# A kernel's own scheduler gets new latencies, transfer costs and priorities, and the last head's probabilities are split straight from PSUM

## The chip, the cores and the metric

One Trainium2 chip, one core. The metric is the time of one execution on the device, in microseconds. The core has TensorE (PE, matmuls and transposes), VectorE (DVE), ScalarE (ACT), GpSimd (POOL), and transfers (DMA), which this kernel starts from SyncE (SP) in one queue.

## The reference

Attention over clusters (2 batches, 8 heads, 768 positions, 64 wide, 16 centroids a head), whose output goes through two feed-forward layers (512 to 2048 to 512, 1536 rows).

```python
# attention
q_assign = argmax(einsum('bhsd,hcd->bhsc', q_n, c_n)); k_assign likewise   # nearest centroid
mask = q_assign[:, :, :, None] == k_assign[:, :, None, :]
scores = where(mask, scale * q @ k.T, -1e9)
scores -= max(scores, -1)
attn = exp(scores);  attn /= sum(attn, -1) + 1e-9
out = attn @ v
# layer 1
h = x @ w_in;  g = maximum(h, 0) + alpha * minimum(h, 0);  x = g @ w_out
# layer 2
h = x @ w_in2
P = a0 + a1*h + a2*h**2 + a3*h**3;  Q = 1 + |b0|*|h| + |b1|*h**2
out = (P / (Q + 1e-6)) @ w_out2
```

The weights arrive as 64-bit floats.

## The kernel before

Every product is made from parts: each operand is split into a high part and what is left of it (low part), and three of the four partial products are added. So each operand needs a copy (high) and a subtraction (low).

*Stages.* Heads i = 0 to 15 come in pairs j = 0 to 7 (i = 2j and 2j+1). For a pair, q, k and v are loaded (`load`), transposed and split (`ph_T`), multiplied with the centroids (`ph_logits`, L552 is the matmul, then `ph_lt`), and made into rows that say which cluster each position has (`ph_oht`). Per head, transfers put the parts together into operand tiles: `operands1` (L617 the q and k parts, L620 and L623 the cluster rows) writes one of 3 slots `op1`, `operands2` (L632, L636) one of 2 slots `op2`. Then:

- `max_chunk`: nine chunks of scores, 512 wide, on PE (L664) into a PSUM bank, DVE takes the row maxima (L670). `m_chain` transposes the maxima on PE (L684) and writes them into `op1` by a transfer (L690).
- `st_chunk`: nine chunks of the transposed scores (PE, L709 and L710) into a bank; ACT takes the exponential (L714) and writes it to a buffer `p32` in SBUF, of which a piece holds two of the six 128-row tiles of P.
- `p_split`: per tile of P, 128x768, the high part (a copy, by ACT L414 or by POOL or DVE L416) and the low part (a subtraction, L726, by DVE or POOL) in `pt`.
- `v_split` (V parts), `pv_tile`: per 128 query rows 18 matmuls (L787 to L789) into a bank of the pool `o`; the first also makes sums of V. `pv_fin` (DVE, L804, L808, L811, L812) normalises, and per pair `x_T` transposes (PE, L826) and splits (ACT; DVE L834) into `x`.

The feed-forward layers are 96 steps of 512 rows by 128 hidden columns: `w_prep` makes weight parts from 64-bit data (L992 and L998 ACT, L1000 and L1002 DVE, L1005 POOL, then a copy and the subtraction L1012), `emit_h` is 12 matmuls (L1029) and the activation, whose parts are L414 and L1075, `emit_y` is 12 more (L1098).

*PSUM.* Eight banks: six (`S`) for chunks of scores and other short uses, two (`o`) for PV, maxima and the like; in the layers four for h, four for y.

*What sets the order.* No engine's order is written by hand. `SC.op(...)` records each operation with the engines that may run it (each with a cost in us, and a bias), what it reads and writes, and a priority `SC.t`, a time in planned us. `Sched.run` then plays through all of them: of the ready operations, each is put on the engine on which it would end first (cost plus bias), and on each engine the one with the smallest start plus `WP` times its priority goes next. A buffer's slot can be taken once its last use has ended by the plan. At the end the instructions are emitted in the order of their planned starts. So a constant in the plan does not delay or speed anything by itself: it sets which instruction stands before which in an engine's queue, and which engine gets an operation that could go to several. On the chip each engine works its queue in that order and waits where something isn't there yet.

Of the kernel before, what the change touches and what calls it, by code (L numbers as in the profile page):

```python
# [19 lines left out]
ACTF = mybir.ActivationFunctionType  # L20
# [10 lines left out]
WP = 0.0025  # L31
# [26 lines left out]
class Sched:  # L58
# [6 lines left out]
    LAT = 0.16  # L65
# [74 lines left out]
    def run(self, engines):  # L140
# [7 lines left out]
        while ready:  # L148
# [42 lines left out]
            if eng == DMA:  # L191
                free[eng] = start + 0.63
                moved = max(moved, start + 1.28) + cost
                o.end = moved + 1.05
            for b in o.bufs:
                b.uses -= 1
                b.done = max(b.done, o.end)
                if b.uses == 0:
                    b.slot.free = b.done
            for x in o.outs:  # L200
                raw = x.deps[o]
                lat = self.LAT
                if eng == DMA:
                    lat = 0.1
                x.est = max(x.est, o.end + lat) if len(x.alts) > 1 or x.alts[0][0] != eng else max(
                    x.est, o.end + (self.SAME if raw and eng != PE else 0.0))
                x.left -= 1
                if not x.left:
                    ready.append(x)
# [44 lines left out]
def clustered_attention__then__ffn_prelu__then__ffn_rational(  # L254
# [64 lines left out]
    EARLY = 77.8906  # L319
    SL, AHEAD, LEAD = 2.0, 14.0, 30.0  # L320
# [117 lines left out]
    def nb(n):  # L438
        return n / 280e3
# [4 lines left out]
    def load(nm, src, j):  # L444
        b, hp = divmod(j, NHP)
        t_ = SC.buf("raw" + nm)
        due = (((2 * j - 1) * T + 1) if nm == "v" else (2 * j - 4) * T + 2) * SL - AHEAD
        whole = nm == "v" or j == 0
        pat = "h (p t) d -> p h t d" if whole else "h (p t) d -> p t h d"
        op((DMA, nb(393216) * (1 if whole else 2)), lambda e: e.dma_start(  # L450
            out=by_head(t_) if whole and nm != "v" else t_.v, in_=src[
                b, 2 * hp:2 * hp + 2].rearrange(pat, t=T)), w=[t_], t=due,
           after=first.get((nm, j), LEAD + due))
        raws[nm, j] = t_
# [200 lines left out]
    def max_chunk(i, c):  # L655
# [11 lines left out]
        op((PE, 0.24), mm, r=[(a, "x"), (a, "oh"), (a, "neg"), (a, "one")], w=[ps])  # L667
# [28 lines left out]
    p32s = {}  # L696

    def st_chunk(i, c):
        a, b_, ps = op1[i % 3], op2[i % 2], SC.buf("S", "st")
        u, cc = divmod(c, CPU)  # L700
        if cc == 0:
            p32s[i, u] = SC.buf("p32")
        p32, parts = p32s[i, u], pieces(cc)

        def mm(e):
            for k_, lo, hi, off in parts:
# [5 lines left out]
        op((PE, 0.48), mm, r=[(b_, 0), (b_, 1), (b_, 2), (a, "x"), (a, "oh"), (a, "neg"),  # L712
                              (a, "one"), (a, "m")], w=[ps])
        op(act_p(CH), lambda e: e.activation(  # L714
# [3 lines left out]
    def p_split(i, t):  # L718
        u, k_ = divmod(t, 2)
# [3 lines left out]
        op([act_s(S), but(dve1(S), 0.5193), but(pool1(S), -0.1128)],  # L723
# [4 lines left out]
        ptile[i, t] = pt_  # L728

# [35 lines left out]
    def pv_tile(i, t):  # L765
# [16 lines left out]
        def mms(e):  # L782
# [8 lines left out]
        op((PE, 0.58), mms,  # L791
           r=[(d, e_, 0), (d, e_, 1), (d, "one")] + [(p, a) for p in tiles for a in range(2)],
# [63 lines left out]
    for i in range(-4, NHEAD + 1):  # L856
        je, jo, jn = (i + 4) // 2, (i + 3) // 2, (i + 2) // 2
        for t in range(T):
            SC.t = (i * T + t) * SL
            if 0 <= i < NHEAD:  # L860
                for c in ((0, 1), (2,))[t % 2]:
                    SC.t = (i * T + t + (0, 0.67, 0.33)[c]) * SL + 0.0
                    st_chunk(i, CPU * (t // 2) + c)
                    if c:
                        SC.t += 0.0 - 0.0
                        p_split(i, t // 2 * 2 + c - 1)
                SC.t = (i * T + t) * SL
# [20 lines left out]
            if i % 2 == 0 and je < NPAIR:  # L888
                if t in (2, 3, 4):
                    hurry(je == 0)  # L890
                    SC.t += 0.0
# [31 lines left out]
            if i >= 3 and i % 2 == 1 and t == 1:  # L923
                SC.t += 3.0579
# [5 lines left out]
    STEP = 5.2  # L930
# [87 lines left out]
    def emit_h(s):  # L1018
# [19 lines left out]
        SC.t = T0 + STEP * (s - 0.0901)  # L1038
# [42 lines left out]
    def emit_y(s):  # L1081
# [21 lines left out]
        for d, (ps, mm) in enumerate(lows):  # L1103
# [4 lines left out]
            SC.t = T0 + STEP * (s - 8.5752)  # L1108
# [60 lines left out]
```

## Time and profile before

| what | before |
|---|---|
| median of 3 runs | 796.49 us (795.05 to 796.76) |
| the profiled execution, its span | 797.74 us, 796.0 us |
| PE busy | 765.4 us, 96% of the span |
| POOL, DVE, ACT busy | 579.7, 599.4, 560.3 us |
| granted clock, mean | 0.984 |
| stages by the span | heads 0 to about 235, the last head's PV beside the first weights to about 271, layers to 787, end 796 |

The span is what the profiler recorded of the execution; 1.74 us lie around it. In the views, a row of the waits says which engine and line waited, for which engine and line (or transfer), how long in all, how often, and the longest. A row of the chain gives the start, the length and what was done. A row of the groups gives the line, engine, operation, output and input with their shapes, the count, the busy time, the mean of one in ns, and the idle time before them.

### The profile page before, as it was taken

The page shows a single profiled execution, that of the slowest core. Times are in us where ns is not written, and L with a number is a line of the kernel's source. Part 1 is how long each engine was busy: PE and PEld are TensorE (multiplying, and loading weights), DVE is VectorE, ACT ScalarE, POOL GpSimd, SP SyncE. Part 2 cuts the span into 40 slices and gives each one's busy share as a digit, 9 for nine tenths or more (in the row PEclk, how much of TensorE's full clock was granted, in tenths as well). Part 3 has the DMA queues.
Part 4 walks back from the last instruction along what each step waited for, and adds up shares of the span by engine and source line. Part 5 has one row for each costly group of instructions (what it writes and reads, how often), then busy time and mean ns, then how long its engine had stood idle before and what let it go on. Part 6 is the DMA issues. An engine that isn't in the chain of part 4 may idle for free.

```text
span 796.0 us, 13977 instructions
## 1 busy us (share of the span) xinstructions
PE 765.4 (96%) x5295; PEld 636.0 (80%) x5295; DVE 599.4 (75%) x871; ACT 560.3 (70%) x991; POOL 579.7 (73%) x475
## 2 busy tenths in 40 slices
PE   8998999999997799999999999999999999999996
PEld 7687797887886688888888888888888888888885
DVE  5787787888797999775662563479889899777775
ACT  3377877887878666665653664688899798666672
POOL 4286956967679899996762773799889689667443
PEclk9899999999899999999999999999999999999999
DMA  5685757656442433332320330211112110000012
GB/s 129 127 171 115 156 126 151 136 123 175 97 102 81 159 99 114 107 108 77 107 80 0 106 96 11 79 54 54 53 54 80 53 54 1 0 1 1 1 54 106
DMA packets 57859, 67.58 MB, mean 85 GB/s; under 512 B 27232, under 2 KB 46272, under 8 KB 57792
## 3 DMA queue, kind: packets, MB, share of 16 engines
q1 hardware_dynamic: 57792, 66.69, 31.9%
q8 instruction: 41, 0.67, 0.4%
q14 instruction: 26, 0.21, 0.1%
HBM read 43.04 MB, written 3.15 MB: 58 GB/s over the span
## 4 chain that ended last, share of the span: by engine, by line
PE 84%; DVE 6%; DMA 5%; ACT 2%; POOL 1%; issue 1%; SPq 1%; DVEq 0%; ACTq 0%; POOLq 0%
PE bank L1029 32%; PE bank L1098 32%; PE bank L709 3%; PE bank L664 3%; PE bank L710 3%; DMA arena_r<-arena_r 2%; PE bank L787 2%; PE bank L552 2%; DVE mp L670 2%; PE bank L789 2%; PE bank L788 2%; DMA arena_p<-in_v 2%; PE bank L525 1%; DMA arena_p<-in_k 1%; DVE arena_p L726 1%
## 5 line engine op out<-in xcount | busy, mean ns | idle before, releaser
L1029 PE MATMUL bank<-x,arena_r 128*128 128x512 f32 x1152 | 277.6, 390 | 3.2 <-ACT arena_r L414 1.1
L1098 PE MATMUL bank<-arena_r 128*128 128x512 f32 x1152 | 277.8, 390 | 1.7 <-ACT arena_r L414 1.0
L1029 PEld LDWEIGHTS bank<-x,arena_r 128*128 128x128 f32 x1152 | 215.9, 188 | 48.9 <-POOL arena_r L1012 3.1
L1098 PEld LDWEIGHTS bank<-arena_r 128*128 128x128 f32 x1152 | 215.6, 188 | 48.4 <-ACT arena_r L414 1.4
L1075 POOL TENSOR_TENSOR arena_r<-arena_p,arena_r 128x512 fp32r<-128x512 f32 x96 | 132.9, 1385 | 38.6 <-ACT arena_r L414 19.8
L726 POOL TENSOR_TENSOR arena_p<-arena_p 128x768 f16<-128x768 f32 x66 | 115.3, 1755 | 18.7 <-ACT arena_p L414 15.1
L414 ACT CAST arena_r<-arena_p 128x512 fp32r<-128x512 f32 x137 | 83.4, 621 | 44.7 <-DVE arena_p L1040 28.1
L1005 POOL TENSOR_TENSOR arena_p<-arena_p 128x512 int32<-128x512 int32 x64 | 93.8, 1468 | 27.1 <-ACT arena_p L998 15.9
L670 DVE TENSOR_REDUCE mp<-bank 128x1 f32<-128x512 f32 x144 | 91.3, 683 | 16.8 <-PE bank L664 16.6
L1012 POOL TENSOR_TENSOR arena_r<-arena_p,arena_r 128x512 fp32r<-128x512 f32 x64 | 92.5, 1447 | 13.0 <-ACT arena_r L414 12.5
L714 ACT ACTIVATE arena_p<-bank 128x512 f32<-128x512 f32 x144 | 80.0, 593 | 30.3 <-PE bank L710 24.4
L1000 DVE TENSOR_SCALAR arena_p<-arena_p 128x512 uint32<-128x512 uint32 x64 | 64.3, 1004 | 38.7 <-ACT arena_p L992 38.7
L1040 DVE SCALAR_TENSOR_TENSOR arena_p<-arena_p,nal 128x512 f32<-128x512 f32 x48 | 53.0, 1106 | 50.2 <-ACT arena_p L1043 50.1
L1002 DVE SCALAR_TENSOR_TENSOR arena_p<-arena_p 128x512 uint32<-128x512 uint32 x64 | 84.1, 1315 | 1.5
L1057 POOL TENSOR_TENSOR arena_p<-arena_p 128x512 f32<-128x512 f32 x48 | 62.4, 1301 | 29.7 <-ACT arena_p L1054 29.5
L709 PE MATMUL bank<-arena_r 128*128 128x512 f32 x192 | 69.8, 381 | 1.4 <-DVE x L834 1.0
L1040 DVE SCALAR_TENSOR_TENSOR arena_p<-arena_p,cq,bank 128x512 f32<-128x512 f32 x48 | 35.7, 744 | 41.8 <-ACT bank L1065 36.1
L789 PE MATMUL bank<-arena_p 128*128 128x65 f16 x576 | 62.2, 197 | 3.6 <-POOL arena_p L726 2.9
L710 PE MATMUL bank<-arena_r 128*128 128x512 f32 x192 | 64.4, 349 | 0.0
L787 PE MATMUL bank<-arena_p 128*128 128x65 f16 x576 | 62.8, 197 | 0.0
L788 PE MATMUL bank<-arena_p 128*128 128x64 f16 x576 | 62.2, 195 | 0.0
L664 PE MATMUL bank<-arena_r 96*128 96x512 f32 x192 | 53.1, 372 | 7.9 <-DMA arena_r<-arena_r 3.5
(122 smaller groups left out, 1272.3 us busy)
## 6 DMA issues: line engine op xcount, KB each, us to landing
arena_p<-in_moe_w_in SPq DMA_DIRECT2D x32, 512.0 KB, 3.8
arena_p<-in_moe_w_out SPq DMA_DIRECT2D x32, 512.0 KB, 3.6
arena_r<-arena_r SPq DMA_DIRECT2D x24, 384.0 KB, 5.4
arena_r<-arena_r SPq DMA_DIRECT2D x24, 192.0 KB, 5.2
arena_p<-in_q SPq DMA_DIRECT2D x8, 384.0 KB
arena_p<-in_k SPq DMA_DIRECT2D x8, 384.0 KB, 5.5
arena_r<-x SPq DMA_DIRECT2D x8, 384.0 KB, 5.5
arena_p<-in_v SPq DMA_DIRECT2D x8, 384.0 KB
```

The source lines that it names most:

```text
L414: e.copy(o_, i_)
L670: op(dvep(CH), lambda e: e.reduce_max(mp.v[:, n0:n0 + 2 * np_ - 1:2], ps.v.rearrange("p (a k) -> p a k", a=np_), axis=AX.X), r=[ps], w=[(m ...
L709: e.matmul(o_, lhsT=b_.v[:, 1, ks], rhs=b_.v[:, 0, lo:hi], start=True, stop=False)
L710: e.matmul(o_, lhsT=a.v[:, 1, ks], rhs=a.v[:, 0, lo:hi], start=False, stop=True)
L726: lambda e: e.tensor_sub(pt_.v[:, 1, :], src(), pt_.v[:, 0, :]),
L1002: op(dve2(N), lambda e, d0=d0, hi=hi: e.scalar_tensor_tensor(u(d0), hi(), 0x80000000, u(d0), op0=ALU.bitwise_and, op1=ALU.bitwise_or), r=[ ...
L1005: op(pool2(N), lambda e, d0=d0, d1=d1: e.tensor_tensor(n32(d0), n32(d0), n32(d1), op=ALU.add), r=[d0, d1], w=[d0])
L1012: lambda e, wt=wt, pick=pick, src=src: e.tensor_tensor(pick(wt.v)[:, 1], src(), f32(pick(wt.v)[:, 0]), op=ALU.subtract),
L1029: e.matmul(ps.v, lhsT=wi.v[:, wi_, kk, :], rhs=x[kk][:, xi, cols], start=n == 0, stop=n == 3 * KD - 1)
L1040: lambda e: e.scalar_tensor_tensor(o_.v, a_.v, sc, b_.v, op0=p0, op1=p1))
L1075: op([dve2(N), pool2(N)], lambda e: e.tensor_tensor(gg.v[:, 1, :], G.v, f32(gg.v[:, 0, :]), op=ALU.subtract), r=[G, (gg, 0)], w=[(gg, 1)])
L1098: e.matmul(ps.v, lhsT=lhsT, rhs=rhs, start=first and wi_ == gi == 0, stop=last and gi == 1)
```

## The change

The plan's constants change, and with them the order: `LAT`, one delay of 0.16 us from the end of an operation to one that needs it on another engine, becomes a part by the engine that ends (`TAIL`) plus a part by the engine that waits (`SEM`). A transfer ends in the plan earlier after its start (1.2 and 0.69 us for 1.28 and 1.05), is moved at 190 in place of 280 KB a us, and the loads that were counted double no longer are. A slot counts as free `TAIL` + 0.09 us after the last use. Costs of three PE operations, the weight of priorities and a number of priority shifts change.

For the last head alone (i = 15), `st_chunk` lets ACT write the exponential back into its PSUM bank; copies (ACT or DVE) and subtractions (DVE) read it there, piece by piece (512 or 256 wide, 12 of each), and `p_split` has nothing to do. The dependences of PV are kept in `pkeys`.

```diff
-WP = 0.0025
+WP = 0.0029
...
-    LAT = 0.16
+    TAIL = {PE: 0.16, ACT: 0.1, DVE: 0.08, POOL: 0.04, DMA: 0.0}
+    SEM = {PE: 0.14, ACT: 0.04, DVE: 0.04, POOL: 0.08, DMA: 0.03}
...
-                moved = max(moved, start + 1.28) + cost
-                o.end = moved + 1.05
+                moved = max(moved, start + 1.2) + cost
+                o.end = moved + 0.69
...
-                b.done = max(b.done, o.end)
+                b.done = max(b.done, o.end + self.TAIL[eng] + 0.09)
...
-                lat = self.LAT
-                if eng == DMA:
-                    lat = 0.1
+                lat = self.TAIL[eng] + self.SEM[x.alts[0][0]]
...
-    EARLY = 77.8906
-    SL, AHEAD, LEAD = 2.0, 14.0, 30.0
+    EARLY = 102.4323
+    SL, AHEAD, LEAD = 2.0, 14.9599, 30.0
...
-        return n / 280e3
+        return n / 190e3
...
-        op((DMA, nb(393216) * (1 if whole else 2)), lambda e: e.dma_start(
+        op((DMA, nb(393216)), lambda e: e.dma_start(
...
-        if cc == 0:
+        if cc == 0 and i < LASTS:
...
+        if i >= LASTS:
...
+            op(act_p(CH), lambda e: e.activation(ps.v, ps.v, ACTF.Exp, scale=scale),
+               r=[ps], w=[ps])
+            for k_, lo, hi, off in parts:
+                t_ = ptile[i, 2 * u + k_]
+                src = lambda off=off, lo=lo, hi=hi: ps.v[:, off:off + hi - lo]
+                op([act_p(hi - lo), dvep(hi - lo)],
+                   lambda e, t_=t_, src=src, lo=lo, hi=hi: copy(e, t_.v[:, 0, lo:hi], src()),
+                   r=[ps], w=[(t_, 0, lo)])
+                op(dvep(hi - lo), lambda e, t_=t_, src=src, lo=lo, hi=hi: e.tensor_sub(
+                    t_.v[:, 1, lo:hi], src(), t_.v[:, 0, lo:hi]),
+                   r=[ps, (t_, 0, lo)], w=[(t_, 1, lo)])
...
+            return
...
     def p_split(i, t):
+        if i >= LASTS:
+            return
...
-        op([act_s(S), but(dve1(S), 0.5193), but(pool1(S), -0.1128)],
+        op([act_s(S), but(dve1(S), 0.5193), but(pool1(S), -0.0486)],
...
-                    SC.t = (i * T + t + (0, 0.67, 0.33)[c]) * SL + 0.0
+                    SC.t = (i * T + t + (0, 0.6098, 0.33)[c]) * SL + 0.0
...
-                        SC.t += 0.0 - 0.0
+                        SC.t += 1.5884 - 0.0
...
-                    SC.t += 0.0
+                    SC.t += 0.8265
                     ph_T(je, t - 2)
...
-                    SC.t += 4.3843
+                    SC.t += 3.2767
                     v_split((i + 1) // 2)
...
-    STEP = 5.2
+    STEP = 5.2741
...
-        SC.t = T0 + STEP * (s - 0.0901)
+        SC.t = T0 + STEP * (s - -0.0819)
...
-            SC.t = T0 + STEP * (s - 8.5752)
+            SC.t = T0 + STEP * (s - 4.2479)
```

The plan is remade as a whole, so instructions move on every engine. Three places, as they stand in the queues; a line's number in the changed kernel is one less up to L710, 19 or 20 more behind it (L726 is L745, L1005 is L1025, L1012 is L1032, L834 is L854).

*SP's queue at the start* (L450 before and L449 after are the loads of q and k, 128x12x64 those of pair 1; L617 or L616 the first transfer of an operand tile). Before:

```order
L450 DMA arena_p<-in_q 128x12x64
L617 DMA arena_r<-x 64x2x768
L450 DMA arena_p<-in_k 128x12x64
L617 DMA arena_r<-x 64x2x768
L620 DMA arena_r<-arena_r 16x768
```

and after:

```order
L449 DMA arena_p<-in_q 128x12x64
L449 DMA arena_p<-in_k 128x12x64
L616 DMA arena_r<-x 64x2x768 x3
L619 DMA arena_r<-arena_r 16x768
L622 DMA arena_r<-arena_r 16x768
```

Pair 1's k load stands ahead of the first operand transfer, and three operand transfers ahead of the first cluster rows.

*PE at pair 3's transposes* (L525 and L524 are the transposes of `ph_T`, L552 and L551 the logits, L590 later transposes of clusters, L775 the sums of V). Before:

```order
L775 LDWEIGHTS level
L775 MATMUL bank<-arena_p,level 128x64
L525 MATMUL bank<-idf,arena_p 128x128 x8
L552 MATMUL bank<-arena_r 128x384 x3
L709 MATMUL bank<-arena_r 128x512
L710 MATMUL bank<-arena_r 128x512
L590 LDWEIGHTS arena_p
```

and after, at the last of these transposes:

```order
L709 MATMUL bank<-arena_r 128x512
L710 MATMUL bank<-arena_r 128x512
L524 MATMUL bank<-idf,arena_p 128x128 x4
L709 MATMUL bank<-arena_r 128x256
L710 MATMUL bank<-arena_r 128x256
L709 MATMUL bank<-arena_r 128x256
L710 MATMUL bank<-arena_r 128x256
```

Before, the logits follow the transposes at once; after, chunks of scores and PV tiles stand between, and the logits come 144 rows of PE's list later.

*POOL and DVE at the last head.* POOL before, from the maxima of head 15 (L681):

```order
L681 TENSOR_SCALAR nh_116<-mx_111 128x6
L726 TENSOR_TENSOR arena_p<-arena_p 128x768 x2
L1005 TENSOR_TENSOR arena_p<-arena_p 128x512
L416 TENSOR_SCALAR arena_r<-arena_p 128x512
L1012 TENSOR_TENSOR arena_r<-arena_p,arena_r 128x512
L1005 TENSOR_TENSOR arena_p<-arena_p 128x512
L726 TENSOR_TENSOR arena_p<-arena_p 128x768
L1012 TENSOR_TENSOR arena_r<-arena_p,arena_r 128x512
L726 TENSOR_TENSOR arena_p<-arena_p 128x768
L1005 TENSOR_TENSOR arena_p<-arena_p 128x512
L726 TENSOR_TENSOR arena_p<-arena_p 128x768
L1012 TENSOR_TENSOR arena_r<-arena_p,arena_r 128x512
```

POOL after, from the same place (L680):

```order
L680 TENSOR_SCALAR nh_116<-mx_111 128x6
L745 TENSOR_TENSOR arena_p<-arena_p 128x768
L1025 TENSOR_TENSOR arena_p<-arena_p 128x512
L415 TENSOR_SCALAR arena_p<-arena_p 128x768
L745 TENSOR_TENSOR arena_p<-arena_p 128x768
L1032 TENSOR_TENSOR arena_r<-arena_p,arena_r 128x512
L745 TENSOR_TENSOR arena_p<-arena_p 128x768
L1025 TENSOR_TENSOR arena_p<-arena_p 128x512
L1032 TENSOR_TENSOR arena_r<-arena_p,arena_r 128x512
L1014 TENSOR_SCALAR arena_p<-arena_p 128x512
L1025 TENSOR_TENSOR arena_p<-arena_p 128x512
```

and DVE after (L726 is here the new subtraction, L824 to L832 the end of PV, L854 the split of x, L1020 and L1022 weights):

```order
L726 TENSOR_TENSOR arena_p<-bank,arena_p 128x256
L854 TENSOR_TENSOR x<-bank,x 128x512
L726 TENSOR_TENSOR arena_p<-bank,arena_p 128x256
L854 TENSOR_TENSOR x<-bank,x 128x256
L1020 TENSOR_SCALAR arena_p<-arena_p 128x512
L726 TENSOR_TENSOR arena_p<-bank,arena_p 128x512
L1022 SCALAR_TENSOR_TENSOR arena_p<-arena_p 128x512
L1020 TENSOR_SCALAR arena_p<-arena_p 128x512
L726 TENSOR_TENSOR arena_p<-bank,arena_p 128x512
L726 TENSOR_TENSOR arena_p<-bank,arena_p 128x256 x2
L1022 SCALAR_TENSOR_TENSOR arena_p<-arena_p 128x512
L726 TENSOR_TENSOR arena_p<-bank,arena_p 128x512
```

The subtractions of the last head's P leave POOL's list, between whose weight splits they stood, and stand as smaller pieces in DVE's, between its weight splits.

More of the change, by code (lines that the diff above doesn't have):

```diff
@@ L665, in mm @@
                          rhs=a.v[:96, 1, lo:hi], start=True, stop=True)
-        op((PE, 0.24), mm, r=[(a, "x"), (a, "oh"), (a, "neg"), (a, "one")], w=[ps])
+        op((PE, 0.23), mm, r=[(a, "x"), (a, "oh"), (a, "neg"), (a, "one")], w=[ps])
         n0 = 6 * u + (0, 1, 4)[c % CPU]
@@ L694, in clustered_attention__then__ffn_prelu__then__ffn_rational @@
     ptile = {}
-    p32s = {}
+    p32s, pkeys = {}, {}
+    LASTS = NHEAD - 1
     def st_chunk(i, c):
@@ L700, in st_chunk @@
         u, cc = divmod(c, CPU)
-        if cc == 0:
+        if cc == 0 and i < LASTS:
             p32s[i, u] = SC.buf("p32")
-        p32, parts = p32s[i, u], pieces(cc)
+        p32, parts = p32s.get((i, u)), pieces(cc)
         def mm(e):
@@ L710, in mm @@
                 e.matmul(o_, lhsT=a.v[:, 1, ks], rhs=a.v[:, 0, lo:hi], start=False, stop=True)
-        op((PE, 0.48), mm, r=[(b_, 0), (b_, 1), (b_, 2), (a, "x"), (a, "oh"), (a, "neg"),
+        op((PE, 0.46), mm, r=[(b_, 0), (b_, 1), (b_, 2), (a, "x"), (a, "oh"), (a, "neg"),
                               (a, "one"), (a, "m")], w=[ps])
+        if i >= LASTS:
+            for k_, *_ in parts:
+                if (i, 2 * u + k_) not in ptile:
+                    ptile[i, 2 * u + k_] = SC.buf("pt")
+            op(act_p(CH), lambda e: e.activation(ps.v, ps.v, ACTF.Exp, scale=scale),
[9 more added lines that the diff above has]
+                   r=[ps, (t_, 0, lo)], w=[(t_, 1, lo)])
+                pkeys.setdefault((i, 2 * u + k_), []).extend([(t_, 0, lo), (t_, 1, lo)])
+            return
         op(act_p(CH), lambda e: e.activation(
@@ L728, in p_split @@
         ptile[i, t] = pt_
+        pkeys[i, t] = [(pt_, 0), (pt_, 1)]
     vinv = {}
@@ L789, in mms @@
                 e.matmul(o1, lhsT=lo, rhs=d.v[:, e_, kt, 64:129], start=False, stop=kt == T - 1)
-        op((PE, 0.58), mms,
-           r=[(d, e_, 0), (d, e_, 1), (d, "one")] + [(p, a) for p in tiles for a in range(2)],
+        op((PE, 0.55), mms,
+           r=[(d, e_, 0), (d, e_, 1), (d, "one")] + [k_ for kt in range(T) for k_ in pkeys[i, kt]],
            w=[(ps, t)])
@@ L898, in clustered_attention__then__ffn_prelu__then__ffn_rational @@
                 hurry(jo == 0)
-                SC.t += (-1.2643, 0, -0.6544, 0, -0.4435, 0)[t]
+                SC.t += (-1.2643, 0, -0.6544, 0, -0.5101, 0)[t]
                 if t == 0:
@@ L923, in clustered_attention__then__ffn_prelu__then__ffn_rational @@
             if i >= 3 and i % 2 == 1 and t == 1:
-                SC.t += 3.0579
+                SC.t += 3.3245
                 x_T((i - 3) // 2)
```

## The prediction

> **What bounds the kernel now.** I read the table by stages first: in the row 280 to 787 TensorE (PE) is busy 506.95 of 507.00 us, so the two FFN layers are bound by PE at full clock, and a new order can only shorten what comes before them, 280 us, and the 9 us behind. Columns: length, busy time of PE, its weight loads, DVE, ACT, POOL, then the granted clock.
>
> ```profile
> 0.00:30.00 30.00, 25.20 (x218) 21.07 (x218) 19.48 (x50) 8.34 (x17) 9.34 (x36) 0.99 0.58 128
> 60.00:120.00 60.00, 55.61 (x719) 47.88 (x716) 48.31 (x92) 45.20 (x88) 42.48 (x35) 0.97 0.61 131
> 180.00:225.00 45.00, 42.23 (x553) 36.35 (x552) 35.53 (x63) 35.12 (x67) 30.24 (x24) 0.92 0.56 131
> 235.40:270.60 35.20, 26.95 (x417) 22.00 (x416) 29.32 (x35) 27.49 (x49) 31.32 (x21) 0.95 0.35 106
> 280.00:787.00 507.00, 506.95 (x2235) 418.73 (x2233) 371.85 (x465) 354.84 (x596) 381.97 (x291) 1.00 0.19 59
> ```
>
> In the heads (60 to 225) PE is still the longest, DVE at 48.31 of 60 has a fifth free. Between 235.4 and 270.6 POOL is the fullest, 31.32 of 35.2, and PE idles 8.25. PE's waits say what to gain. The first two rows are of 0 to 60, then five of 60 to 236, then the longest of 236 to 280 and the only one of 780 to 796 (us in all, times, longest):
>
> ```profile
> PE bank L664 <- DVE mp L670: 2.0, 3, 0.8
> PE bank L525 <- DMA arena_p<-in_k: 0.8, 1, 0.8
> ...
> PE bank L664 <- DMA arena_r<-arena_r: 3.5, 3, 1.8
> PE bank L552 <- DMA arena_r<-x: 2.0, 1, 2.0
> PE bank L684 <- DVE arena_p L575: 1.7, 1, 1.7
> PE bank L664 <- ACT arena_r L530: 1.6, 1, 1.6
> PE bank L590 <- DVE arena_p L812: 0.5, 1, 0.5
> ...
> PE bank L789 <- POOL arena_p L726: 2.9, 1, 2.9
> ...
> PE bank L1098 <- ACT arena_r L414: 1.0, 1, 1.0
> ```
>
> Last, where PE ran at half clock:
>
> ```profile
> 97.61:101.02 3.41, 3.41 (x30) 3.10 (x29) 1.89 (x3) 0.55 (x2) 2.74 (x2) 0.50 0.00 0
> 200.01:206.83 6.82, 6.82 (x63) 6.24 (x59) 5.05 (x11) 5.54 (x12) 3.56 (x4) 0.50 0.00 0
> 264.86:268.27 3.41, 2.73 (x51) 2.74 (x52) 3.34 (x4) 1.35 (x3) 2.72 (x3) 0.50 0.49 154
> ```
>
> Work in such a stretch takes twice as long, so a stretch of 3.41 costs about 1.7 and one of 6.82 about 3.4.
>
> **The change, part by part.** Prices of PE, from the chain of waits at full clock: a 512-wide matmul .24 or a little less (so a score chunk .23, a transposed one .47), the 18 matmuls of a PV tile .56 (229.00 to 229.56).
>
> ```profile
> 228.30 0.24 PE bank L710
> ...
> 229.00 0.05 PE bank L787
> ...
> 229.56 0.32 PE bank L664
> ```
>
> *Start (new constants for transfers).* The k load of pair 1 goes ahead of head 0's operand transfers. Before, it was issued at 10.05, behind a 0.65 us issue that waited for ACT, and landed at 16.95; DVE's row of maxima ends this stage.
>
> ```profile
> 9.36 0.65 SPq L617
> 10.05 6.90 DMA arena_p<-in_k
> 22.35 4.28 DVE mp L670 x7
> ```
>
> Queued behind q instead, the 6.90 us are over long before 16.95, so the wait of .8 goes; the three waits of 2.0 for the maxima go only as far as DVE starts earlier. What is late next is head 0's own operands, now third in that queue. I take −1.0, between 0 (DVE ends it anyway) and −2.8 (both rows).
>
> *Heads, waits that go.* I counted what PE has between a step and the one that needs it. From the last transposed chunk of head i−3, which frees the operand slot, to the first score chunk of head i: for head 6, before 7 transposed + 3 score + 4 PV + 1 small step, 6.1 us; now 8 + 3 + 7 + 2, 8.5. Head 10 goes from 6.1 to 9.3, head 14 from 7.4 to 9.0. Added, +2.4, +3.2 and +1.6; the three waits of that kind (3.5 in all, 1.8 the longest) fit inside: −3.5. The wait of 2.0 at L552 is put down to a DMA, but the chain has DVE's low part of the transposes ending just there (63.16 + .59 = 63.75):
>
> ```profile
> 63.16 0.59 DVE arena_r L532
> ```
>
> Before, the logits of pair 3 follow its transposes at once; now 6 score chunks, 4 PV tiles (one of sums), 2 transposed chunks lie between, 4.3 us: −2.0. The waits of 1.7 (maxima of head 12; 4.45 us of PE work before it, and still) and 1.6 (operand slot of head 8; 15.6 to 15.7) stay.
>
> *Heads, waits that come.* The transposes of pair 6's output now have .7 us of PE work between them and the PV tile they depend on, before 2.7. What has to happen between is L804, L808, L811, L812, 1.53 in all by the rows below: +1.0 with the handovers. And PV of a head starts sooner after its last transposed chunk: head 4 8.0 to 4.6, 6 6.9 to 4.2, 10 10.6 to 4.2, 13 5.4 to 3.6, 14 8.9 to 4.7; heads 7 and 5 get longer.
>
> ```profile
> L714 ACT ACTIVATE arena_p<-bank 128x512 f32<-128x512 f32 x144 | 80.0, 593 | 30.3 <-PE bank L710 24.4 <-issue 3.1 <-PE bank L664 1.4
> L414 ACT CAST arena_p<-arena_p 128x768 f16<-128x768 f32 x65 | 53.0, 835 | 0.5
> L726 POOL TENSOR_TENSOR arena_p<-arena_p 128x768 f16<-128x768 f32 x66 | 115.3, 1755 | 18.7 <-ACT arena_p L414 15.1 <-PE bank L684 1.5
> L726 DVE TENSOR_TENSOR arena_p<-arena_p 128x768 f16<-128x768 f32 x30 | 35.0, 1167 | 10.8 <-ACT arena_p L414 6.9 <-POOL arena_p L416 3.8
> L804 DVE COPY_PREDICATED bank<-nh,bank 128x390 f32<-128x390 uint32 x16 | 9.0, 562 | 5.5 <-PE bank L789 5.5
> L808 DVE TENSOR_SCALAR rc<-bank,am 128x6 f32<-128x6 f32 x16 | 3.5, 221 | 0.1
> L811 DVE RECIPROCAL rc<-rc 128x6 f32<-128x6 f32 x16 | 3.0, 190 | 0.4
> L812 DVE TENSOR_TENSOR arena_p<-bank,rc 128x384 f32<-128x384 f32 x16 | 8.9, 556 | 0.5
> ```
>
> Exp, high part and POOL's low part add to .59 + .84 + 1.76 = 3.2, and to 4.9 if POOL has another subtraction first. Head 5 stood at 3.8 before, and no PV line is in the list of waits of 60 to 236; so I take +.5 for heads 13, 6 and 10 together, between 0 and +4 (the five to 4.9: .3 + .7 + .7 + 1.3 + .2, and a handover each). Heads in all −3.5 − 2.0 + 1.0 + .5 = −4.0. Lower bound −9.3 (all five rows gone), upper 0.
>
> *Half clock in the heads.* The stretch at 97.61 begins behind one of the slot waits that go:
>
> ```profile
> 91.82 5.29 DMA arena_r<-arena_r
> 97.24 1.31 PE bank L664 x4
> ...
> 198.67 0.27 PE bank L684
> ```
>
> The one at 200.01 follows the wait for head 12's maxima, which stays. I take −1.0 (1.7, not certain), between −5.1 and +3.4 (one of the longer kind appears). [...]
>
> *Last head (P parts read from PSUM).* POOL loses four subtractions, by its row 4 × 1.755 = 7.0; DVE takes twelve that read PSUM, and two it had from SBUF go. Nothing before is that operation; the nearest rows are the first two, DVE subtractions from a bank (the other two are its weight splits):
>
> ```profile
> L532 DVE TENSOR_TENSOR arena_r<-bank,arena_r 128x512 fp32r<-128x512 f32 x18 | 11.9, 683 | 2.8 <-ACT arena_r L530 2.7
> L834 DVE TENSOR_TENSOR x<-bank,x 128x256 fp32r<-128x256 f32 x8 | 3.3, 414 | 0.0
> L1002 DVE SCALAR_TENSOR_TENSOR arena_p<-arena_p 128x512 uint32<-128x512 uint32 x9 | 12.7, 1413 | 0.2
> L1000 DVE TENSOR_SCALAR arena_p<-arena_p 128x512 uint32<-128x512 uint32 x9 | 11.6, 1288 | 0.5 <-ACT arena_p L992 0.5
> ```
>
> Six of 512 and six of 256 make 6 × .683 + 6 × .414 = 6.6. Before, PE waits 2.9 for the last P part, which POOL ends at 265.49 (263.43 + 2.06), behind its weight splits:
>
> ```profile
> 263.43 2.06 POOL arena_p L726
> ```
>
> DVE's list from the last maxima (235.4) to the last new subtraction: 6.6, three subtractions of head 14 (3.5), one handover of PV (1.5), the output of pair 6 (1.1), and four weight splits (4 × (1.29 + 1.41) = 10.8), 23.5 and so about 259, 6 us before 265.5. Given back: DVE, not POOL, now ends the stage, and its list has no free time left; PV of head 15 and the output of pair 7 come behind two weight splits in DVE's order (+1.4), and PE has a long idle ahead of head 14's PV (+1.4, most of what a stretch of 3.41 costs). 6 − 2.8 = 3.2 saved. Bounds: PE's idle of 8.25 is all there is to gain; and if DVE's splits slow it by a third, about +2 lost. ACT's twelve copies from PSUM, at L714's .593 for 512 and between half and all of it for 256, are 5.3 to 7.1 against 6 × .835 = 5.0; ACT has 7.7 of 35.2 free, so nothing (2.1 without that cover). A bank is held until its copies and subtractions are done, but six are there for scores and no head follows: nothing, or one more subtraction of .68 if all six fill.
>
> *End, and the rest.* In the last steps ACT does the next piece first, −.3 of the 1.0 us wait (bounds −1.0, +.3). Weight copies moved from ACT to POOL and the like in 280 to 787 cost nothing: PE there waits for nobody, and POOL has 125 of 507 us free; would that cover go, 18 copies at the .84 of ACT's row for a larger one are 15 us at most.
>
> Sum: −1.0 − 4.0 − 1.0 − 3.2 − .3 = −9.5. The profiled execution took 797.74, so 788.2; it stands 1.25 above the median of 796.49, so 787.0.
>
> **The rivals.**
> 1. *All of it goes*: with the waits both stretches go (−5.1 for −1.0) and the last head gives 6 for 3.2. 787.0 − 4.1 − 2.8 = 780. For it: both stretches begin right after a wait. Against: the wait at 198.67 has no more cover than before.
> 2. *The waits only move.* Where PE no longer waits for a slot it waits for DVE (81% busy) a few chunks later, and in the last head DVE's 23.5 us lead to the same end. Only the start and .3 remain: about 795.5.
> 3. *Slower: the P parts come late.* If the five PV starts need 5.9 (4.9 and 1.0 of queue), they wait 29.5 − 21.3 = 8.2 in all, and if three of those waits bring a half-clock stretch (1.7 each), that is 8.2 + 5.1 less the .5 counted: 787.0 + 12.8, about 800. It decides from about 9.5 us of it. Against: head 5.
> 4. *The long idle.* Ahead of head 14's PV PE has no work for about 5 us; if that brings the long stretch of 6.82, +3.4 less the 1.4 counted, and the DVE list lasts 3 longer: 792. [...] The stretch at 264.86, which begins inside the 2.9 wait, shows that a shorter one can be enough.
>
> **How the numbers follow.** Forecast 787 (its own range 783 to 791) .50; rival 1 .15; rival 2 .12; rival 3 .13; rival 4 .10. A measurement of this kernel tells about 0.2%, 1.6 us, from no change: faster is below 794.9, slower above 798.1. Faster: .50 + .15 + .10 and .02 of rival 2, less .01, .76; same: .10 of rival 2; slower: rival 3 and the .01, .14. Range 778 to 800: rival 1 and 2 us for its spread, rival 3.
>
> **What would show it.** Right: the list of PE's waits has no DMA at the score chunks (L664, L663 after) and no wait at the logits of pair 3; DVE's subtractions from a bank take .68 and .41; the first FFN products begin about 9 us earlier, and from there to the end the time is that of before. Wrong: PV lines in that list before 236, more or longer stretches at .50, DVE without a gap from the last maxima to the first FFN products, or any wait inside the FFN.

## The result, and the profile after

The changed kernel takes 771.43 us (median of 4 runs, 769.66 to 771.93) beside 795.77 (4 runs, 794.75 to 796.76): ratio 0.969, 95% interval 0.9669 to 0.9712, 24.3 us less. The forecast was 787.0, 9.5 us less, with a range of 778 to 800: the direction was right, the measured change is 2.6 times the forecast one, and the time lies outside the range. The profiled execution took 771.93, span 770.1, so 25.8 of span are to be explained.

The stages of the changed kernel, columns as before. The fourth row is the last head (from the end of its row maxima to the third FFN step), which in the kernel before lay at 235.43 to 270.64:

```profile
0.00:30.00 30.00, 26.16 (x223) 22.07 (x223) 19.69 (x51) 8.33 (x17) 9.37 (x36) 1.00 0.59 129
60.00:120.00 60.00, 59.04 (x826) 51.78 (x826) 51.59 (x94) 52.69 (x103) 46.90 (x39) 1.00 0.70 150
180.00:225.00 45.00, 43.56 (x649) 38.07 (x648) 42.30 (x80) 41.02 (x80) 37.57 (x30) 1.00 0.59 133
217.35:244.46 27.11, 24.23 (x409) 20.92 (x406) 25.38 (x41) 25.36 (x53) 23.15 (x19) 1.00 0.46 142
244.46:761.00 516.54, 514.83 (x2275) 425.13 (x2272) 392.35 (x479) 350.93 (x593) 412.01 (x321) 1.00 0.19 61
```

The heads end at 217.35 in place of 235.43 (18.1 earlier), the last head takes 27.1 in place of 35.2 (8.1 less), and what follows takes 525.7 in place of 525.3. PE does the same work in each part. So I count what it loses: the length less the sum of its matmuls, each at about the shortest distance to the next that its shape shows at full clock (235 ns for 96x512, 226 for 128x512, 29 for the 65 wide ones of PV). Heads: 49.4 lost before, 31.6 now, of which in half clock 10.6 and 1.8. Last head: 12.8 and 5.1, in half clock 2.0 and 0. FFN and end: 10.1 and 10.1. This is a count from one trace of each kernel; what half clock costs in time is tried in experiment 5.

PE's waits in the heads now, up to 217.3 (14.8 us in all before, 6.2 now), then the longest of those behind:

```profile
PE bank L868 <- DVE mp L650: 2.0, 1, 2.0
PE bank L709 <- DVE mp L669: 1.1, 1, 1.1
PE bank L663 <- DVE mp L669: 0.9, 2, 0.6
PE bank L663 <- ACT arena_p L731: 0.9, 1, 0.9
PE bank L809 <- DVE arena_p L745: 0.2, 1, 0.2
...
PE bank L793 <- DVE arena_p L832: 1.7, 1, 1.7
PE bank L846 <- DVE arena_p L726: 0.8, 1, 0.8
PE bank L1118 <- POOL arena_r L415: 0.9, 1, 0.9
```

No score chunk (L663) waits for a transfer any more, and no logits for their transposes: both named ahead. L809 (PV waiting for a P part) is 0.2 in one place, and L868, 2.0, stands at the very start as before (L848 there). Of the five stretches of half clock before the last microseconds, 23.9 us, one is left, here with the window ahead of it:

```profile
27.49:30.91 3.42, 2.43 (x13) 1.29 (x12) 3.42 (x7) 1.05 (x2) 0.00 (x0) 1.00 0.32 89
30.91:34.32 3.41, 3.41 (x11) 2.61 (x12) 2.96 (x6) 2.35 (x8) 0.94 (x2) 0.50 0.91 214
```

### The profile page after: what moved, and what is told of

The parts are those of the page before. It is cut to its first block, busy times and chain, and to the rows that moved or that the text cites. A ratio compares the mean times of both kernels' runs of the same rounds, so it can differ in the third digit from the quotient of the medians.

```text
span 770.1 us, 13979 instructions
## 1 busy us (share of the span) xinstructions
PE 753.7 (98%) x5295; PEld 631.1 (82%) x5295; DVE 608.5 (79%) x881; ACT 545.8 (71%) x975; POOL 588.2 (76%) x493
## 4 chain that ended last, share of the span: by engine, by line
PE 60%; DVE 20%; POOL 9%; ACT 8%; issue 2%; DVEq 0%; POOLq 0%; ACTq 0%
PE bank L1118 19%; PE bank L1049 19%; DVE arena_p L1060 6%; PE bank L709 4%; PE bank L663 4%; PE bank L710 3%; POOL arena_p L1077 3%; DVE arena_p L1137 3%; DVE mp L669 2%; POOL arena_r L1095 2%; PE bank L551 2%; DVE bank L1060 2%; ACT bank L1085 2%; PE bank L807 1%; ACT arena_p L1083 1%
## 5 line engine op out<-in xcount | busy, mean ns | idle before, releaser
L1095 POOL TENSOR_TENSOR arena_r<-arena_p,arena_r 128x512 fp32r<-128x512 f32 x96 | 136.0, 1419 | 37.3 <-ACT arena_r L413 30.6
L745 POOL TENSOR_TENSOR arena_p<-arena_p 128x768 f16<-128x768 f32 x61 | 105.8, 1740 | 14.2 <-ACT arena_p L413 11.3
L1025 POOL TENSOR_TENSOR arena_p<-arena_p 128x512 int32<-128x512 int32 x64 | 91.0, 1426 | 17.7 <-DVE arena_p L1022 7.7
L1060 DVE SCALAR_TENSOR_TENSOR arena_p<-arena_p,nal 128x512 f32<-128x512 f32 x48 | 59.0, 1231 | 56.7 <-ACT arena_p L1063 56.5
L413 ACT CAST arena_r<-arena_p 128x512 fp32r<-128x512 f32 x120 | 72.7, 619 | 42.0 <-DVE arena_p L1060 27.5
L1032 POOL TENSOR_TENSOR arena_r<-arena_p,arena_r 128x512 fp32r<-128x512 f32 x64 | 94.8, 1486 | 3.5 <-ACT arena_r L413 2.1
L731 ACT ACTIVATE arena_p<-bank 128x512 f32<-128x512 f32 x135 | 75.1, 594 | 15.8 <-PE bank L710 11.2
L1022 DVE SCALAR_TENSOR_TENSOR arena_p<-arena_p 128x512 uint32<-128x512 uint32 x64 | 83.3, 1302 | 1.4
L1020 DVE TENSOR_SCALAR arena_p<-arena_p 128x512 uint32<-128x512 uint32 x64 | 64.6, 1010 | 21.6 <-ACT arena_p L1012 21.4
L1083 ACT ACTIVATE arena_p<-arena_p,cq 128x512 f32<-128x512 f32 x48 | 34.9, 726 | 40.6 <-POOL arena_p L1077 40.4
L710 PE MATMUL bank<-arena_r 128*128 128x512 f32 x192 | 62.6, 341 | 0.0
L807 PE MATMUL bank<-arena_p 128*128 128x65 f16 x576 | 60.0, 193 | 0.0
L809 PE MATMUL bank<-arena_p 128*128 128x65 f16 x576 | 59.3, 194 | 0.2 <-DVE arena_p L745 0.2
L808 PE MATMUL bank<-arena_p 128*128 128x64 f16 x576 | 59.5, 192 | 0.0
```

The costliest lines, as they stand in the source:

```text
L710: e.matmul(o_, lhsT=a.v[:, 1, ks], rhs=a.v[:, 0, lo:hi], start=False, stop=True)
L745: lambda e: e.tensor_sub(pt_.v[:, 1, :], src(), pt_.v[:, 0, :]),
L1022: op(dve2(N), lambda e, d0=d0, hi=hi: e.scalar_tensor_tensor(u(d0), hi(), 0x80000000, u(d0), op0=ALU.bitwise_and, op1=ALU.bitwise_or), r=[ ...
L1025: op(pool2(N), lambda e, d0=d0, d1=d1: e.tensor_tensor(n32(d0), n32(d0), n32(d1), op=ALU.add), r=[d0, d1], w=[d0])
L1032: lambda e, wt=wt, pick=pick, src=src: e.tensor_tensor(pick(wt.v)[:, 1], src(), f32(pick(wt.v)[:, 0]), op=ALU.subtract),
L1060: lambda e: e.scalar_tensor_tensor(o_.v, a_.v, sc, b_.v, op0=p0, op1=p1))
```

## The experiments

Twenty profiled kernels in all, grouped by question. "New times" are the plan's latencies, transfer times, slot handover and PE costs; "priorities" the rest of the constants. The kernel before, run beside each group, had medians of 793.6 to 795.5. Gains given for one kernel are to the one beside; where two changed kernels are compared, their medians are subtracted as they stand, which that spread of about 2 us bears on.

| kernel | median, us | ratio to before (95%) | mean clock | PE waits 60 to 225 |
|---|---|---|---|---|
| before | 795.8 | 1 | .988 | 9.5 |
| changed | 771.4 | .969 (.967 to .971) | .997 | 1.1 |
| last head alone | 790.6 | .996 (.994 to .999) | .990 | 8.6 |
| changed, without last head | 780.3 | .984 (.980 to .987) | .992 | 2.1 |
| new times alone | 785.7 | .990 (.987 to .994) | .986 | 0.3 |
| priorities alone | 800.7 | 1.009 (1.007 to 1.012) | .984 | 8.8 |
| transfer times alone | 792.3 | .997 (.996 to .999) | .980 | 6.0 |
| latencies and handover alone | 802.2 | 1.010 (1.007 to 1.012) | .981 | 11.2 |
| new times + last head | 779.7 | .981 (.979 to .983) | .986 | 0 |

(The clock is the mean over a kernel's runs, for the kernel before over the 78 runs beside the others; its profiled execution had .984. The waits are the sum of the list in the profile.)

**1. The parts.** The last head alone (`LASTS = NHEAD - 1` and what hangs on it, old constants):

> The kernel before, with the change of the last head alone (exponential back into PSUM, 12 copies and 12 subtractions from there), all of the plan's constants as before. Theory A (in the last head POOL's list set the end, and taking four subtractions out of it is worth what the two traces differ between head 14's last PV tile and head 15's, 25.1 - 17.7 = 7.4 us): about 788 to 790, and PE's wait of 2.9 us for POOL gone. Rival B (DVE's list takes POOL's place, the gain there came from the new order): 794 to 798.

790.6: between the two. The wait for POOL's subtraction is gone, but waits take its place, the longest of 225 to 285:

```profile
PE bank L847 <- DVE arena_p L727: 1.4, 1, 1.4
PE bank L1050 <- POOL arena_r L1033: 1.3, 1, 1.3
PE bank L1119 <- ACT arena_r L414: 0.9, 1, 0.9
```

And the reverse, with all new constants:

```diff
-    LASTS = NHEAD - 1
+    LASTS = NHEAD
```

> The changed kernel without the change of the last head: all new constants, but P of head 15 goes through SBUF as before. Theory A: 771.4 + 7.4, about 779, heads up to 14 as in the changed kernel. Rival B: 771 to 773.

780.3, so the last head is worth 8.9 us beside the new order (11.0 if each is taken against the kernel before beside it), 3.0 beside the old one, and 6.0 (7.3) between new times alone and new times with it. Without it PE loses 12.9 us between 225 and 282, where 10.2 us of the time are at half clock; with it PE loses 4.5, and none of it is at half clock. Theory A holds beside the new order.

New times alone, and priorities alone (the lines of the diff for each, nothing else):

> The kernel before with the plan's latencies, transfer times, slot handover and PE costs of the change; priorities, weights and biases as before; last head as before. Theory C (the order of the heads got better because the plan now knows when operands and slots are there): most of the 17.7 us of the heads, 779 to 785, with the waits of PE for operand transfers and slots gone and at most one stretch of half clock between 30 and 230 us. Rival D (the new priorities did it): 792 to 800, with waits of 1 us and more still there.

> The kernel before with the new priorities, their weight and the biases alone; latencies and transfers of the plan as before, last head as before. Theory C: 792 to 800. Rival D: 779 to 785. If both this and the run with the new latencies alone stay near 796, the two need each other, or any new order would have been as good.

The waits of PE in the heads with new times alone, all that is left of 9.5 us, and then its longest in the last head:

```profile
PE bank L663 <- ACT arena_r L529: 0.3, 1, 0.3
...
PE bank L788 <- POOL arena_p L725: 3.3, 1, 3.3
PE bank L1028 <- ACT arena_r L413: 2.4, 1, 2.4
PE bank L1028 <- POOL arena_r L1011: 2.1, 1, 2.1
```

So theory C is right on what it names: the new times take the waits out of the heads (PE loses 16.3 us there between 60 and 225 against 30.4). It is off in the time, 785.7, since 3 us go back at the start and in the last head. Priorities by themselves cost 7 us; D falls.

**2. Which times.**

```diff
-                moved = max(moved, start + 1.28) + cost
-                o.end = moved + 1.05
+                moved = max(moved, start + 1.2) + cost
+                o.end = moved + 0.69
...
-        return n / 280e3
+        return n / 190e3
...
-        op((DMA, nb(393216) * (1 if whole else 2)), lambda e: e.dma_start(
+        op((DMA, nb(393216)), lambda e: e.dma_start(
```

These lines alone, and in a second kernel `TAIL`, `SEM` and the handover of slots alone; the costs of PE are in neither.

> The kernel before with the plan's transfer times of the change alone (1.2 and 0.69 us, 190 KB a us, no doubling). Theory I (the operand waits went because transfers queue longer in the plan): waits of PE for operand transfers between 60 and 225 us gone, 3.5 us down to under 1, the time 786 to 790. Rival J (they went by latencies between engines and the slots' handover): waits as before, 792 to 798.

> The kernel before with the plan's latencies by engine and the later handover of slots alone. Theory I: operand waits as before, 792 to 798. Rival J: waits of 60 to 225 us down to under 2 in all (9.5 before), 784 to 788, about as with all the plan's new times (785.7).

PE's longest waits between 60 and 225: first with transfer times alone, then with latencies alone:

```profile
PE bank L684 <- DVE arena_p L812: 3.2, 1, 3.2
PE bank L664 <- DMA arena_r<-arena_r: 0.4, 1, 0.4
...
PE bank L663 <- DMA arena_r<-arena_r: 3.6, 2, 2.0
PE bank L663 <- ACT arena_p L713: 3.5, 2, 2.0
```

I holds on the waits: the operand waits go with the transfers' times (3.5 to 0.4), not with the latencies (3.6). It is off in the time: 792.3 is what J said. In their place a wait of 3.2 for a slot that DVE frees stands, which is gone with all the new times. So each half alone leaves long waits: the halves make -2.6 and +7.2 us, both together (and the PE costs) -7.9.

**3. New times and the last head, old priorities.**

> The kernel before with all new times of the plan and the change of the last head, priorities as before. Theory K (the parts of the change do different things in different places, and add up where they meet no new wait): 785.7 less the 7 to 9 us that the last head was worth beside the new order, 777 to 779, the start still with the waits of 3.6 us that the run with new times alone had. Rival L (without the new priorities the last head gains only the 3.0 us that it gained alone): 782 to 784.

779.7, K to within 1. From there to the changed kernel 8 us are left for the priorities, though alone they cost 7. I first looked for one of them in the changed kernel: the P splits' priority, that of the transposes, the weight of priorities.

```diff
-                        SC.t += 1.5884 - 0.0
+                        SC.t += 0.0 - 0.0
```

> The changed kernel with the priority of the P splits as before (no 1.59 later). Theory M (this constant lets the short steps of the maxima and of the clusters go ahead of 1.2 to 1.8 us subtractions on DVE; in the kernel before, one of 1.39 stood between the two steps that free the bank for head 12's maxima): waits of PE for DVE's L574 to L579 or L832 come back between 60 and 225 us, 775 to 779. Rival N (with the plan's times right, no single priority matters much): 770 to 773.

788.5 (ratio .9925, .990 to .995): 17 us lost, far more than M said, with 6.7 us of waits between 60 and 225 and 13.7 us of half clock there. DVE then has a P subtraction ahead of row maxima that stood first; the first place where its order differs (+ stands in this kernel alone, - in the changed one):

```text
 L745 TENSOR_TENSOR arena_p<-arena_p 128x768
 L669 TENSOR_REDUCE mp_114<-bank 128x1
+L745 TENSOR_TENSOR arena_p<-arena_p 128x768
+L531 TENSOR_TENSOR arena_r<-bank,arena_r 128x512 x2
 L669 TENSOR_REDUCE mp_114<-bank 128x2
 L669 TENSOR_REDUCE mp_114<-bank 128x1
-L531 TENSOR_TENSOR arena_r<-bank,arena_r 128x512 x3
+L531 TENSOR_TENSOR arena_r<-bank,arena_r 128x512
```

and PE waits for maxima and for a step of the clusters (L574), as M said:

```profile
PE bank L663 <- DVE mp L669: 2.8, 3, 1.7
PE bank L760 <- DVE arena_p L574: 1.1, 1, 1.1
```

```diff
-                    SC.t += 0.8265
+                    SC.t += 0.0
                     ph_T(je, t - 2)
```

> The changed kernel with the priority of the transposes as before (no 0.83 later). Theory M: transposes stand closer to their logits again, waits of 0.5 to 2 us for DVE's low parts (L531) come back at some pairs, 773 to 777. Rival N: 770 to 773.

```diff
-WP = 0.0029
+WP = 0.0025
```

> The changed kernel with the weight of priorities as before (0.0025). PE's queue changes in 18 rows, DVE's in 208, ACT's in 186. Theory M: it only swaps neighbours, 770.5 to 773. Rival O (the order is a lottery in which a small move can cost a wait with a stretch of half clock behind it): 774 to 780.

774.0 (.9736) and 772.4 (.9719). The first has the transposes' clusters (L589) waiting 1.8 and one stretch of half clock, not the waits that I expected; the second is the changed kernel within what can be told. So most depends on the P splits' priority. Is it that one constant?

> The kernel before with the plan's new times, the last head and, of all priorities, only that of the P splits (1.59 later). Theory P (this one constant, with right times, puts DVE's row maxima ahead of its long subtractions; the other priorities matter little): 770 to 775. Rival Q (the priorities work as a set): 778 to 788.

> The kernel before with the P splits' priority 1.59 later and nothing else. Theory P, and with old times as well: 780 to 790. Rival Q: 794 to 803, as with all priorities and the old times (800.7).

> The changed kernel with the P splits' priority 3.0 later in place of 1.59. Theory P: 770 to 775, since the maxima stand ahead already, with a wait or two of PE for late P parts. Rival T (every later is better): 765 to 769. Rival Q: 776 and more, as a new lot of the order.

788.3 (.991), 795.0 (1.000) and 787.3 (.990): no. With new times and the other priorities old it costs 8.6 us, and a later one in the changed kernel costs 16. Q holds: the priorities work as a set, and what one of them does alone can't be told ahead: moved back in the changed kernel, the three cost 0.9, 2.6 and 17 us. The ten kernels with all new times and nothing else put in lie at 771 to 789, those with old ones, or half of the new, at 791 to 802.

**4. Two heads from PSUM** (`LASTS = NHEAD - 2`):

> The changed kernel with P read from PSUM for the last two heads instead of one. Theory R (the gain comes from POOL having weights to split beside the last head; in head 14 a PSUM bank that waits for two subtractions on DVE is missing to the next scores): 772 to 778. Rival S (what helps in one head helps in two): 765 to 770.

773.4 (.9726, .970 to .975), a time as R said: head 15's maxima now wait 1.8 us for a bank (L683 for DVE's L832, the end of a PV, which stands behind new subtractions in DVE's list), and 6.83 us of half clock follow. It is the maxima that wait, not the scores that R named.

**5. Half clock.** The largest surprise, so its cause was tried directly: work put into the waits, in the same order.

```diff
+    FILL = {("max", 6, 0): 30, ("m", 12): 30, ("max", 1, 6): 10, ("max", 1, 7): 8, ("max", 2, 3): 12}
...
+    def fill(e, n):
+        for _ in range(n):
+            e.matmul(bank[:, 7, 480:512], lhsT=idb, rhs=idb[:, :32], start=True, stop=True)
...
+            fill(e, FILL.get(("max", i, c), 0))
```

> The kernel before, same order on every engine, with small matmuls of constants (32 wide, into PSUM columns that nobody reads) put on PE right ahead of five of its waits: 10 and 8 ahead of score chunks 6 and 7 of head 1, 12 ahead of chunk 3 of head 2, 30 ahead of the first chunk of head 6, 30 ahead of the maxima of head 12. No wait becomes shorter. Theory G (half clock is brought on by PE standing still in those waits, though each is under 2 us): the four stretches of half clock between 29 and 207 us go, up to 20.5 / 2 = 10 us less than before. Rival H (the clock has other reasons, or a wait's own length is all it costs): the same time as before, or up to 1 us more.

> As the first run with small matmuls in PE's waits, but more of them, since 30 took only 0.56 us of a 1.78 us wait there: 25 and 20 ahead of chunks 6 and 7 of head 1, 30 ahead of chunk 3 of head 2, 75, 60, 30 and 30 ahead of the first chunks of heads 6, 8, 10 and 14, 70 ahead of head 12's maxima, some 19 ns each. Theory G (half clock comes from PE standing still): the mean granted clock rises from .987 to .993 or more, and 4 to 8 us go. Rival H: mean clock .985 to .989, time within 2 us of before, or longer by what the matmuls overshoot.

797.0 (1.003, 1.0015 to 1.0047) and 795.3 (1.001, .999 to 1.0025). In the first profile the stretches behind the two longer fills are gone, but the mean clock over the runs stayed at .988; with more of them it rose to .991, and the time did not fall. Neither as G said, nor quite as H. But the first profile shows what a stretch costs where PE sets the pace. From the maxima of head 12 to those of head 13 the order and the work are the same; before, the stretch at 200.01 lies in it, with the small matmuls ahead it doesn't:

```profile
198.67:212.52 13.85, 13.85 (x132) 11.87 (x133) 11.40 (x24) 11.98 (x23) 8.27 (x8) 0.75 0.32 65
198.99:210.05 11.06, 10.98 (x131) 9.02 (x132) 10.74 (x24) 10.93 (x23) 7.60 (x7) 1.00 0.43 93
```

So 6.83 us of half clock cost 2.8 us there; in the second kernel the same way takes 10.94 us. Over the runs the first kernel had as much half clock as the kernel before (.988 both), and in the second's profile new stretches stand at 59.74 and 155.32; that the second's rise to .991 gave no time is put down here to what the matmuls cost, which was not tried apart. Runs of one kernel differ as well: of the 78 of the kernel before, the 16 with a mean clock of .985 or less have a median of 796.2 us, the 32 with .989 or more one of 792.8. The profiled one, at .984, has more half clock than most.

The busy share didn't tell here which window comes ahead of half clock. Of these four of the kernel before, the first and the last two are followed by it and the second is not:

```profile
25.93:29.34 3.41, 2.00 (x8) 1.05 (x7) 3.38 (x9) 0.27 (x1) 0.23 (x1) 1.00 0.23 49
60.06:63.47 3.41, 1.67 (x22) 1.34 (x20) 3.41 (x6) 1.46 (x3) 2.44 (x3) 1.00 0.98 213
94.19:97.61 3.42, 1.64 (x40) 1.49 (x39) 0.64 (x1) 3.42 (x9) 3.19 (x3) 1.00 0.67 136
196.59:200.01 3.42, 1.73 (x19) 1.04 (x18) 3.25 (x5) 3.39 (x8) 3.42 (x4) 1.00 0.00 0
```

Counted as work at full-clock prices (eight matmuls of the first window fill 28% of it, though they show busy for 59%), it tells better, though not in the middle: by that count the second and the third of these four both hold about 41%. In 18 profiled executions (those without 32 wide matmuls), from 15 to 285 us, cut at the 3.41 us steps at which the clock changes, of the windows at full clock: under 40% of work, 41 of 44 were followed by half clock; from 40 to 55%, 19 of 63; from 55% on, none of 1229. The last two kernels were made from that reading, before they were counted in:

```diff
+    FILL = {(i, c): 5 for i in range(3) for c in range(NCH)}
...
+            for _ in range(FILL.get((i, c), 0)):
+                e.matmul(ps.v[:, :P], lhsT=idb, rhs=idb, start=True, stop=True)
             for b_, lo, hi, off in ps_:
```

(For the kernel with new times, last head and old priorities; there 34 more stand ahead of the sums of V of head 0. For the changed kernel `FILL` is 5 for chunks 3 to 8 of head 1 alone.)

> The kernel with new times, the last head and old priorities (779.7 us, mean clock .986), with five matmuls of constants (128 wide, 56 ns each) ahead of each score chunk of heads 0 to 2 and 34 ahead of the sums of V of head 0, in banks that the next product overwrites. There DVE's maxima set the pace, one chunk of .235 us of PE work in .68 us. Theory U (a window of 3.41 us in which PE has work for less than about 40% is followed by half clock; there are 17 us of it between 25 and 49 us): with .235 + .28 of work in .68 us the windows stay over 55%, the stretches go, mean clock .993 or more, 771 to 774. Rival V (the clock has other reasons, or the fillers cost what they bring): 779 to 784.

> The changed kernel with five such matmuls ahead of chunks 3 to 8 of head 1. Theory U: its only stretch before the end (3.41 us at 30.9, behind a window with 41% of work) goes, 1.7 us less, 769 to 770.5. Rival V: 771 to 773.

The kernel with new times, last head and old priorities: its two stretches at the start, and then 0 to 30 and 30 to 60 with the small matmuls:

```profile
25.24:32.07 6.83, 6.45 (x22) 4.25 (x22) 6.79 (x14) 1.85 (x3) 0.26 (x1) 0.50 0.40 110
38.89:49.13 10.24, 7.39 (x53) 6.63 (x52) 7.53 (x13) 5.72 (x12) 4.34 (x4) 0.50 0.93 185
...
0.00:30.00 30.00, 27.82 (x286) 24.88 (x287) 19.44 (x50) 8.06 (x16) 9.32 (x36) 1.00 0.59 127
30.00:60.00 30.00, 28.60 (x317) 24.39 (x315) 21.75 (x40) 22.84 (x47) 16.37 (x15) 1.00 0.80 164
```

U is right on the cause: 17 us of half clock are gone at the start. On the worth it is V that holds: 781.8 us (.9825) beside 779.7, so the matmuls cost at least what they brought. In the profiles the maxima of head 0 come 3.7 us later with them, those of head 1 2.4 and those of head 2 1.0 later; so part of what the matmuls delay is won back, but not all. Another part of the 2.3 us between the two profiles lies at the last head, where half clock now lasts 6.83 us in place of 3.41. Between head 0's and head 2's the way is 2.7 us shorter, so half clock cost something there; what the 17 us alone are worth is left open. In the changed kernel the small matmuls gave a clock of 1.000 in the profile and 770.3 us (.968, .966 to .970), which can't be told from its .969. The stretch of 3.41 us at its start is gone, and head 2's maxima come 0.1 us earlier (54.74 and 54.84). DVE is the busiest engine at the start (6.79 of 6.83 us in the first stretch above), so a PE at half clock may cost little there; but these times hold the cost of the small matmuls too, and the two were not told apart.

## Why the forecast was wrong, step by step

The places and the waits named ahead were right in the main. Three terms of the sum were too small: the waits of the start and the heads (5.0 said, 8.6 measured), half clock (1.0 said, up to 8.8) and the last head (3.2 said, 8.1).

- *What bounds it, and where it can change*: right. FFN and end 525.3 and 525.7; the end wait 1.0 and 0.9 (-0.3 was said).
- *Start, -1.0*: the wait for the k load is gone, but head 0's first transposed chunk starts at 30.16 (29.88 before). As named, DVE ends that stage.
- *Heads, waits, -4.0*: with the start they fell by 8.6 (14.8 to 6.2), where 5.0 was said. The operand and logits waits went as counted. Wrong is the step that let the waits of 1.7 and 1.6 stay because PE's queue has the same work ahead of them. That counts the waiting engine only. The bank for head 12's maxima is freed by a step on DVE (L575), which before stood behind a P subtraction (L726) that waited 1.6 us for its high part, a copy on POOL:

```profile
196.76 1.39 DVE arena_p L726
198.15 0.48 DVE arena_p L575
198.67 0.27 PE bank L684
...
186.13 0.11 PE bank L683
```

(Three pieces of the chain before, one after.) DVE now does the two steps of the clusters one behind the other, and PE goes on without a wait. How the wait of 1.6 went was not traced. The waits put on top, 1.0 for pair 6's output and 0.5 for P parts, came as 0.8 (L846, behind the last maxima) and 0.2.
- *Half clock, -1.0*: this is the term most mis-sized. PE lost 10.6 us to it in the heads before, 1.8 after, so up to 8.8 went with the waits. I had priced only the two stretches at 97.61 and 200.01, at half the length of each as if the work in them took twice as long (PV's 65 wide matmuls start 54 ns apart in both, 29 at full clock; the 128x512 ones at the shortest 426 ns apart in the second, 226 at full clock: 1.9 times), left out the two at the start, and took the chance of their going too low: the second went with the wait that I let stay. Between 60 and 225, where these two lie, PE lost 5.2 to half clock before and nothing after; experiment 5 shows 2.8 us of time for the longer one. The rest of the 8.8 lies at the start, where its worth in time is open, and the trace before is one with more half clock than most, so 8.8 is an upper bound. The bound of -5.1 counted two of four stretches. The two at the start, before:

```profile
29.34:36.17 6.83, 6.44 (x22) 4.40 (x21) 5.17 (x10) 3.13 (x5) 2.37 (x2) 0.50 0.76 176
42.99:46.41 3.42, 3.42 (x23) 3.13 (x23) 3.39 (x7) 2.71 (x6) 2.50 (x2) 0.50 1.19 204
```

- *Last head, -3.2*: 8.1. The new subtractions took what the nearest rows said, .680 and .408 (.683 and .414 said):

```profile
L726 DVE TENSOR_TENSOR arena_p<-bank,arena_p 128x512 f16<-128x512 f32 x6 | 4.0, 680 | 0.5 <-ACT arena_p L413 0.5
L726 DVE TENSOR_TENSOR arena_p<-bank,arena_p 128x256 f16<-128x256 f32 x6 | 2.3, 408 | 0.0
238.03 1.34 DVE arena_p L726 x3
239.97 0.60 DVE arena_p L726
```

The last ends at 240.57, 23.2 us behind the last maxima (23.5 said; POOL's before 30.1). That this came so close is in part luck: DVE's weight splits there, L1020 and L1022, took 8.8 where 10.8 was said, and the three subtractions of head 14 took 4.3 where 3.5 was said. Wrong is the 2.8 taken off again. The long idle ahead of head 14's PV did not come (waits of 1.7 at L793, then 0.8 and 0.3) and no half clock either, pair 7's output waits 0.8 (L846 for L832), and the 2.0 lost to half clock there before are gone.
- *Rivals*: 1 ("all of it goes") was the case, but at 780 it still gave 8.6 us less than was measured, because its bounds were the two stretches and the list of waits as I had sorted it. 3 and 4 did not come about: PV waits 0.2 in the heads, and the idle of 4 brought no stretch. In the kernel before, half clock came behind short gaps too: the stretch at 97.61 stands behind a gap of 1.8 us, the one at 200.01 behind one of 1.7, and the one at 29.34 behind a window (25.93) whose gaps are all under 0.7.

What is open: why the set of priorities is worth 8 us beside new times and costs 7 beside old ones was not taken apart further; nor why windows of 40 to 55% go either way; nor how much of the 24.3 us is half clock and how much the waits ahead of it.

## What to carry to other kernels

When a planner's numbers change, compare the queue of the engine that frees the buffer, not only the queue of the one that waits. A wait of 1.7 us on a path that PE sets was followed here by half clock that cost 2.8 more, so list the stretches at half clock and ask of each whether its cause goes. Give the planner new times of all kinds at once (transfers alone -2.6, latencies alone +7.2, together with PE's costs -7.9), then retune priorities as a set, since one moved alone cost anything from 1 to 17 us here.

## What the runs showed of the hardware

Before the last microseconds, the granted clock was 0.50 in stretches of 3.41, 6.83 and 10.24 us, one, two and three times 3.41. Counted as in experiment 5 (15 to 285 us, 18 executions), of the windows of 3.41 us at full clock that held under 40% of matmul work, 41 of 44 were followed by half clock; of those with 40 to 55%, 19 of 63; of those with 55% or more, none of 1229.

The maxima of head 0 alone lie near 40%. DVE took the nine in 5.47 us (21.15 to 26.62 in the kernel before, 21.44 to 26.91 in the changed one), one each 0.61 us, and PE's matmul work for each is 0.235 at full clock, 39% of that. In the kernel with new times and last head the window 21.83 to 25.24 holds about 51% with the other work in it, and half clock follows; at half clock PE then shows as busy for 6.45 of 6.83 us.

6.83 us of half clock where PE sets the pace, from head 12's maxima to head 13's, cost 2.8 us (13.85 us with it, 11.06 without).

The subtraction of a 768 wide P tile from SBUF took 1.17 us on DVE and 1.76 on POOL in the mean (the kernel before); from PSUM DVE did the same width in 0.680 + 0.408 = 1.09 us (the changed kernel). POOL has no part in that here.
